# Zero fills of a decode backward kernel: waiting for the query weight instead of the output weight

## The chip, the cores and the metric

The kernel runs on one core of a Trainium2 chip. The metric is the device time of one execution in microseconds (us), as the median of several executions. Of the kernel before, three runs were known at first (765.28 to 765.92 us, median 765.66); more were taken later beside every experiment, on the same chip as that experiment. A run more than 1.5% above the fastest of the same kernel is called slow, and comparisons use the other (fast) runs alone.

## The reference, cut to what matters

The program is forward and backward of a decode step: layer norm, attention over the last 4096 positions of a 32768-long cache, multiplied by a gated feed-forward branch. It returns the output and nine gradients.

```python
k_cache, v_cache: bf16 [2, 8, 32768, 128]
W = 4096                                     # only the last W positions are attended to
k = k_cache[:, :, Sk - W:, :]; v = v_cache[:, :, Sk - W:, :]
s = attention(xn @ wq, k, v) @ wo            # xn = layernorm(x)
g = silu(square(relu(xn @ w1 + b1)) @ w2 + b2)
out = x + s * g
return out, gradients for (x, k_cache, v_cache, wq, wo, w1, b1, w2, b2)
```

What matters is the size of the outputs. The gradients of both caches are 134 MB each, and seven eighths of each is exact zero, because only the last 4096 of 32768 positions were used. The kernel therefore has to write some 235 MB of zeros, beside about 46 MB of other outputs and 46 MB of inputs.

## The kernel before

The zeros come from one zeroed tile `zt` in on-chip memory. There are 32 zero areas (2 gradients, 2 batch entries, 8 heads), each of 28672 x 128 bf16, 7.34 MB. GpSimd issues 31 of them through its software DMA queue ("fills"), and SyncE issues the last one at the very end.

```python
ZR = SK - W                                   # 28672 zero rows per area
def zf(o, q, r0, nent, rows, rep=1):          # one fill: nent partitions, rows rows per packet
    ...
    sw_fill.append(nc.gpsimd.dma_start(out=v, in_=zs))

zlong = (0, 1, 3, 5, 7, 11, 12, 16, ..., 30)  # these areas go in packets of 224 rows = 57344 B
zshort = {2: (...), 4: (...), ...}            # eight areas cut by hand into smaller pieces
...
for qi in range(ZQ - 1):
    r = 0
    whole = (P, ZR // P, 1) if qi in zlong else (P, ZG, ZR // (P * ZG))   # 57344 B or 28672 B
    for n, rows, rep in zshort.get(qi, (whole,)):
        r = zf(*zparts[qi], r, n, rows, rep)
```

The loads are issued by SyncE, in this order, and the first fill waits for one of them:

```python
dma_load.dma_start(out=w1, ...)                        # 1.8 MB, feed-forward weights
dma_load.dma_start(out=w2, ...)                        # 1.8 MB
wo_in = dma_load.dma_start(out=wo[:], ...)             # 4.2 MB, output weight
dma_load.dma_start(out=wq[:], ...)                     # 4.2 MB, query weight
vnat = load(A_v_cache, 0, "v")                         # 4.2 MB, first V tile
# ... the fills are issued here, by GpSimd ...
for f in sw_fill:
    tc.add_manual_dep(f.ins, wo_in.ins.name, ...)      # every fill waits for wo
```

The compute chain is: layer norm, feed-forward branch, transposes of `wo`, queries (the first use of `wq`), then four rounds. A round uses a V tile and a K tile of 4.2 MB each; their gradients overwrite them in place and are stored by ScalarE's DMA queue, and only after that store has landed can the next V or K tile be loaded into the same memory. So loads, stores and compute of the rounds form one long chain. The first K load waits for compute to have read `w1` and `w2`, whose memory it takes. The end:

```python
dma_store.dma_start(out=out_5..., in_=wo[:])           # gradient of wo
...
nc.sync.dma_start(out=out_8..., in_=dw2_st)
...
last = nc.sync.dma_start(out=out_6..., in_=dw1_st)     # last result of compute, 1.8 MB
with tc.issue_after(last.ins):
    fin = nc.sync.dma_start(out=v, in_=zs)             # the 32nd zero area, 7.34 MB
tc.add_manual_dep(fin.ins, sw_fill[-2].ins.name, ...)  # and it waits for the last fill but one
```

Of the kernel before, what the change touches and what calls it, by code (L numbers as in the profile page):

```python
# [16 lines left out]
def kernel(  # L17
# [34 lines left out]
    DK = D // P  # L52
    NJ = N // P
# [14 lines left out]
    dma_load = nc.sync  # L68
# [104 lines left out]
    wq = wts.tile([P, DK, N], BF16, name="wq")  # L173
    wo = wts.tile([P, NJ, D], BF16, name="wo")
# [33 lines left out]
    def load(src, r, tag):  # L208
        nat = kvp.tile([P, NCB * DH], BF16, tag=tag)
        dma_load.dma_start(out=nat[:], in_=kv_of(src, r))  # L210
        return nat[:].rearrange("p (c d) -> p c d", d=DH)

    with tc.tile_pool(name="pw", bufs=1) as pw:
# [7 lines left out]
        dma_store.dma_start(out=b2_bf[:], in_=B_b2.rearrange("(p k) -> p k", k=DK))  # L221
        dma_load.dma_start(out=w1, in_=B_w1.rearrange("(p k) f -> p k f", k=DK))
        dma_load.dma_start(out=w2, in_=B_w2.rearrange("(p j) d -> p j d", j=FK))
        wo_in = dma_load.dma_start(out=wo[:], in_=A_wo.rearrange("(p j) m -> p j m", j=NJ))
        dma_load.dma_start(out=wq[:], in_=A_wq.rearrange("(p k) n -> p k n", k=DK))
        vnat = load(A_v_cache, 0, "v")
        for qi in range(ZQ - 1):
            r = 0
# [2 lines left out]
                r = zf(*zparts[qi], r, n, rows, rep)  # L231
            assert r == ZR
        for f in sw_fill:
            tc.add_manual_dep(f.ins, wo_in.ins.name,
                              mybir.DependencyInfo(mybir.DependencyClass.Sync, mybir.DependencyReason.DATA))

        tp = ps_m.tile([P, DK, B], BF16, tag="m")
# [66 lines left out]
        for j0 in range(0, NJ, JG):  # L304
            woT = pw.tile([P, JG, DK, P], BF16, tag="woT", bufs=2)
            for half in range(2):
                tp = ps_t.tile([P, 8, P], BF16, tag="pt")
                for jj in range(8):
                    j, dk = divmod(half * 8 + jj, DK)
# [31 lines left out]
        for g0 in range(0, len(jobs), 8):  # L341
# [4 lines left out]
            j = 0  # L346
            while j < len(grp):
                dst, idx, off = grp[j][1], grp[j][2], grp[j][3]
                n = 1
# [83 lines left out]
    for r in range(NR):  # L433
# [122 lines left out]
        for hk in range(h0, h0 + NP) if b == B - 1 else ():  # L556
            xps = ps_m.tile([P, DK, B], F32, tag="m")
            for half in range(2):
                wqT = wsl.tile([P, 2, DK, P], BF16, tag="wqT")
                tp = ps_t.tile([P, 8, P], BF16, tag="pt")  # L560
                for jj in range(8):
                    i, k = divmod(half * 8 + jj, DK)
# [51 lines left out]
    for k in range(DK):  # L614
        for n0 in range(0, F, 512):
            n = min(512, F - n0)
# [58 lines left out]
```

## Time and profile before

| | before |
|---|---|
| median of the first three runs | 765.66 us |
| span of the profiled run | 764.6 us |
| bytes moved, mean rate | 326.73 MB, 427 GB/s |
| first fill issued | 23.1 us |
| last result of compute handed to the DMA | 696.9 us |
| last fill issued (by SyncE) | 724.2 us |

The first lines are from the page: the span, the busy times, the shares of the span in 40 equal slices (a digit is tenths; the GB/s row is the rate of each slice), the totals, and the DMA queues (packets, MB, share of the 16 engines).

```profile
span 764.6 us, 9391 instructions
...
PE 388.6 (51%) x4109; PEld 234.4 (31%) x4118; DVE 275.8 (36%) x483; ACT 214.9 (28%) x313; POOL 34.7 (5%) x67
...
DMA  9999999999999999999999999999999999999998
GB/s 378 434 410 428 447 420 425 442 438 414 437 423 435 429 435 431 426 433 425 430 430 445 430 422 438 422 436 424 440 442 430 430 425 432 432 427 428 442 409 367
DMA packets 12217, 326.73 MB, mean 427 GB/s; under 512 B 2898, under 2 KB 2906, under 8 KB 2934
...
q0 software_dynamic: 7744, 227.55, 70.3%
q1 hardware_dynamic: 2696, 56.63, 20.8%
q10 hardware_dynamic: 1736, 41.95, 13.9%
```

The DMA row has no hole, and from the 2nd to the 38th of the 40 slices the rate stays between 410 and 447 GB/s. q0 is the fills, q1 what SyncE issues (loads, some stores, the last fill), q10 what ScalarE issues (stores). No compute engine is near its limit. The view of stretches says the same of the end; its columns are the stretch, its length, busy time (and instructions) of PE, PE's weight loads, VectorE, ScalarE and GpSimd, then the granted clock, the DMA share and GB/s (a transfer counts where it starts, so a share can pass 1):

```profile
700.00:745.00 45.00, 0.00 (x0) 0.00 (x0) 0.00 (x0) 0.00 (x0) 0.00 (x0) 0.50 1.02 427
745.00:760.00 15.00, 0.00 (x0) 0.00 (x0) 0.00 (x0) 0.00 (x0) 0.00 (x0) 0.50 1.01 433
```

For the last 60 us no compute engine does anything, and the pipe (here: the 16 DMA engines taken together) is full almost to the end. So compute ends long before the kernel does.

The wait that the change moves is in the view of waits of GpSimd (who waited for whom: us in total, times, longest):

```profile
POOL out_dram L101 <- DMA out_dram<-zt: 507.8, 39, 27.3
...
POOL out_dram L101 <- DMA wo<-in_A_wo_dram: 21.4, 1, 21.4
```

The first line is the normal course of the fills: each new one waits for room behind an earlier one. The second is the wait for `wo` at the start. In the timeline (start us, us, engine, line, operation) the first eight fills follow at once, and the end is in SyncE's queue:

```profile
23.08 4.83 POOL L101 DMA_DIRECT2D out_dram<-zt  x8 [21.43 <-DMA wo<-in_A_wo_dram]
...
696.91 0.33 SPq L639 DMA_DIRECT2D out_dram<-dw  x1
724.24 0.39 SPq L644 DMA_DIRECT2D out_dram<-zt  x1
```

The DMA view gives KB of one transfer and the median us from issue to landing:

```profile
out_dram<-nat ACTq DMA_DIRECT2D x8, 4096.0 KB, 40.5
...
nat<-in_A_v_cache_dram SPq DMA_DIRECT2D x4, 4096.0 KB, 31.8
nat<-in_A_k_cache_dram SPq DMA_DIRECT2D x4, 4096.0 KB, 26.6
...
wq<-in_A_wq_dram SPq DMA_DIRECT2D x1, 4096.0 KB, 41.2
```

The query weight was issued at 2.2 us (timeline) and landed 41.2 us later, at about 43.4 us, because from 27.5 us on it shared the engines with fills.

### The profile page before, as it was taken

What the parts mean: (1) busy time and instruction counts of PE and PEld (TensorE: products, weight loads), DVE (VectorE), ACT (ScalarE), POOL (GpSimd) and SP (SyncE); (2) the same over time, 40 slices, a digit from 0 to 9 for tenths busy, and PEclk for the clock granted to TensorE, in tenths of its full rate; (3) what the DMA queues carried; (4) which work ended last, traced back from release to release, by engine and by line L of the source; (5) the groups of instructions that cost most, each with busy time, mean ns of one, the idle gap of its engine ahead of it and who ended that gap; (6) DMA issues with size and microseconds to landing.
All of it is one profiled execution on the core that took longest, in us unless ns stands there. A gap on an engine that the chain in (4) does not pass through costs nothing.

```text
span 764.6 us, 9391 instructions
## 1 busy us (share of the span) xinstructions
PE 388.6 (51%) x4109; PEld 234.4 (31%) x4118; DVE 275.8 (36%) x483; ACT 214.9 (28%) x313; POOL 34.7 (5%) x67
## 2 busy tenths in 40 slices
PE   0566774477007747830784770038459467594000
PEld 0543553333005534410463320026344333321000
DVE  3234342485003446430554650014344245663000
ACT  0044521455001246530224550002422254153000
POOL 0200100010000000000000000000000000000000
PEclk9986997778556867665596775559859666555555
DMA  9999999999999999999999999999999999999998
GB/s 378 434 410 428 447 420 425 442 438 414 437 423 435 429 435 431 426 433 425 430 430 445 430 422 438 422 436 424 440 442 430 430 425 432 432 427 428 442 409 367
DMA packets 12217, 326.73 MB, mean 427 GB/s; under 512 B 2898, under 2 KB 2906, under 8 KB 2934
## 3 DMA queue, kind: packets, MB, share of 16 engines
q0 software_dynamic: 7744, 227.55, 70.3%
q1 hardware_dynamic: 2696, 56.63, 20.8%
q10 hardware_dynamic: 1736, 41.95, 13.9%
q8 instruction: 32, 0.52, 0.3%
q14 instruction: 9, 0.07, 0.0%
HBM read 45.62 MB, written 280.50 MB: 427 GB/s over the span
## 4 chain that ended last, share of the span: by engine, by line
DMA 32%; PE 31%; DVE 13%; ACT 9%; issue 6%; ACTq 0%; SPq 0%; DVEq 0%
DMA out_dram<-nat 14%; DMA nat<-in_A_v_cache_dram 8%; DMA nat<-in_A_k_cache_dram 7%; PE tp L387 6%; PE ov L421 5%; ACT tring L150 3%; DMA b_bf<-in_B_b_dram 2%; ACT p_bf L455 2%; ACT nat L150 2%; DVE tring L152 2%; PE s_ps L394 2%; DVE nat L152 2%; DVE ds_bf L468 2%; PE wps L588 2%; PE dops L314 2%
## 5 line engine op out<-in xcount | busy, mean ns | idle before, releaser
L387 PE MATMUL tp<-pperm,nat 128*128 128x128 bf16 x1024 | 91.9, 243 | 144.7 <-DMA nat<-in_A_v_cache_dram 126.5
L152 DVE COPY tring<-tp 128x1024 bf16<-128x1024 bf16 (+1 forms) x98 | 65.9, 689 | 179.1 <-PE tp L387 169.4
L387 PEld LDWEIGHTS <-nat 128*128 128x128 bf16 x1024 | 68.5, 109 | 165.1 <-DMA nat<-in_A_v_cache_dram 128.4
L150 ACT CAST nat<-ov 128x512 bf16<-128x512 f32 x160 | 87.7, 589 | 68.8 <-PE ov L421 48.1
L150 ACT COPY tring<-tp 128x1024 bf16<-128x1024 bf16 (+1 forms) x34 | 34.4, 1011 | 228.5 <-PE tp L387 155.1
L152 DVE CAST nat<-ov 128x512 bf16<-128x512 f32 x96 | 65.6, 690 | 59.7 <-PE ov L421 57.1
L101 POOL DMA_DIRECT2D out_dram<-zt x58 | 33.1, 576 | 529.3 <-DMA out_dram<-zt 507.8
L421 PE MATMUL ov<-bd,ds_bf 128*128 128x512 bf16 x124 | 49.4, 472 | 6.6 <-DVE nat L152 3.9
L421 PE MATMUL ov<-bd,p_bf 128*128 128x512 bf16 x123 | 47.3, 451 | 5.5 <-DVE nat L152 1.4
L410 PE MATMUL ps<-t,nat 128*128 128x16 bf16 x1024 | 28.7, 173 | 14.3 <-DVE bd L375 7.2
L410 PEld LDWEIGHTS <-nat 128*128 128x128 bf16 x1024 | 28.7, 103 | 17.1 <-issue 11.9
L394 PEld LDWEIGHTS <-zz 128*32 128x32 bf16 x512 | 17.8, 96 | 33.4 <-issue 23.1
L152 DVE CAST wq<-wps 128x512 bf16<-128x512 f32 x16 | 11.0, 690 | 42.4 <-PE wps L581 42.3
L402 PE MATMUL tp<-ident_bf,p_bf 128*128 128x128 bf16 x64 | 7.6, 312 | 34.9 <-ACT p_bf L455 34.9
L394 PE MATMUL s_ps<-tring,zz 128*32 128x256 bf16 x256 | 19.2, 288 | 11.8 <-ACT tring L150 7.4
L394 PE MATMUL dp_ps<-tring,zz 128*32 128x256 bf16 x256 | 20.5, 326 | 7.1 <-ACT tring L150 4.2
L150 ACT CAST wq<-wps 128x512 bf16<-128x512 f32 x16 | 9.4, 586 | 51.7 <-PE wps L581 51.7
L455 ACT ACTIVATE p_bf<-e_sb,rl 32x512 bf16<-32x512 f32 x16 | 22.8, 1424 | 3.4 <-DVE rl L452 3.2
L468 DVE SCALAR_TENSOR_TENSOR ds_bf<-dp_ps,delta,p_bf 32x512 bf16<-32x512 f32 x16 | 21.7, 1355 | 0.2
L421 PEld LDWEIGHTS <-ds_bf 128*128 128x128 bf16 x128 | 13.1, 110 | 20.6 <-issue 18.3
L421 PEld LDWEIGHTS <-p_bf 128*128 128x128 bf16 x128 | 12.9, 110 | 19.6 <-issue 16.7
L564 PE MATMUL tp<-ident_bf,wq 128*128 128x128 bf16 x128 | 16.8, 248 | 2.3 <-issue 2.3
(195 smaller groups left out, 435.5 us busy)
## 6 DMA issues: line engine op xcount, KB each, us to landing
out_dram<-zt POOLq DMA_DIRECT2D x23, 7168.0 KB, 100.0
out_dram<-nat ACTq DMA_DIRECT2D x8, 4096.0 KB, 40.5
out_dram<-zt POOLq DMA_DIRECT2D x7, 3584.0 KB, 71.3
nat<-in_A_v_cache_dram SPq DMA_DIRECT2D x4, 4096.0 KB, 31.8
nat<-in_A_k_cache_dram SPq DMA_DIRECT2D x4, 4096.0 KB, 26.6
out_dram<-zt SPq DMA_DIRECT2D x1, 7168.0 KB, 39.5
out_dram<-zt POOLq DMA_DIRECT2D x2, 3488.0 KB, 66.9
out_dram<-zt POOLq DMA_DIRECT2D x1, 6120.0 KB, 67.6
```

Of the source, the lines that this page charges most:

```text
L101: sw_fill.append(nc.gpsimd.dma_start(out=v, in_=zs))
L150: nc.scalar.copy(out=out_ap, in_=in_ap)
L152: nc.vector.tensor_copy(out=out_ap, in_=in_ap)
L314: nc.tensor.matmul(dops[0:B, :, :], lhsT=dsT_bf[:, dk, :], rhs=woT[:, :, dk, :], start=(dk == 0), stop=(dk == DK - 1))
L387: nc.tensor.transpose(tp[:, j, :], nat[:, g * CC + half * CH + j, :], pperm[:].rearrange("p b k -> p (b k)"))
L394: nc.tensor.matmul(out_ps[pr * RB:(pr + 1) * RB, half * CH * PB:(half + 1) * CH * PB], lhsT=zbuf[:, pr, o:o + RB], rhs=tT[:, :, pr, :], st ...
L410: nc.tensor.matmul(ps[:], lhsT=nat[:, g * CC + half * CH + cc, :], rhs=cols[half][:, cc, :, g, :], start=(half == 0 and g == 0 and cc == 0 ...
L421: nc.tensor.matmul(ov[:], lhsT=src[:, cc].rearrange("r k b -> r (k b)"), rhs=bd[:, gh * 4:(gh + 1) * 4, :], start=True, stop=True)
L455: nc.scalar.activation(out=p_bf[rb, :, :, pr], in_=e_sb[rb], func=ACT.Copy, scale=rl[rb, 0:1])
L468: nc.vector.scalar_tensor_tensor(out=ds_bf[rb, :, :, pr], in0=dp_c[rb], scalar=delta[rb, 0:1], in1=p_bf[rb, :, :, pr], op0=ALU.subtract, o ...
L564: nc.tensor.transpose(tp[:, jj, :], wq[:, k, n0:n0 + DH], ident_bf[:, :])
L588: nc.tensor.matmul(wps[:], lhsT=o_rows[:, j:N:NJ], rhs=ds_rows[:, :], start=True, stop=True)
```

## The change

The intent is to let one more load have the pipe to itself before the flood of zeros starts. One wait moves; no instruction is added, removed or reordered on any engine.

```diff
-        wo_in = dma_load.dma_start(out=wo[:], in_=A_wo.rearrange("(p j) m -> p j m", j=NJ))
-        dma_load.dma_start(out=wq[:], in_=A_wq.rearrange("(p k) n -> p k n", k=DK))
+        dma_load.dma_start(out=wo[:], in_=A_wo.rearrange("(p j) m -> p j m", j=NJ))
+        wq_in = dma_load.dma_start(out=wq[:], in_=A_wq.rearrange("(p k) n -> p k n", k=DK))
         vnat = load(A_v_cache, 0, "v")
 ...
         for f in sw_fill:
-            tc.add_manual_dep(f.ins, wo_in.ins.name,
+            tc.add_manual_dep(f.ins, wq_in.ins.name,
                               mybir.DependencyInfo(mybir.DependencyClass.Sync, mybir.DependencyReason.DATA))
```

## The prediction

> **What bounds the kernel now.** The DMA engines, from the first microseconds to the last. The page shows the DMA row at 9 tenths in 39 of 40 slices, and 326.73 MB at a mean 427 GB/s: 326.73 MB / 427 GB/s = 765 us, the whole span (764.6). Compute is far from that: PE 51%, VectorE 36%, ScalarE 28%. The view of stretches shows every compute engine at zero from 700 us on, while the DMA keeps moving 400 to 443 GB/s until 750 us. The chain of waits is mixed (DMA 32%, PE 31%) and doesn't set the end: the last store (a 7168 KB zero fill issued by SyncE at 724 us) shares a full pipe. The Trainium skill, "DMA: Bandwidth & Descriptors", section "Issuing engines are not separate DMA queues", says that transfers started by any engine run on the same 16 DMA engines and interleave; the trace agrees: the total stays near 430 GB/s whichever queues are active.
>
> **What the change does.** No instruction is added, removed or reordered; one semaphore wait before the first GpSimd fill moves from the output weight to the query weight. Before, GpSimd waited 21.4 us for the output weight and issued its first fill at 23.1 us; fill data moved from about 27.5 us. From there fills shared the engines with the loads of the query weight (landed at about 43 us, 2.2 + 41.2) and the first V tile (65 to 75 us).
>
> After, loads keep the engines alone longer, at about 425 GB/s: the query weight (12.06 MB of loads in all) should land near 32 us, the first fill be issued at 32 to 34 us, fill data start at 36 to 38 us, and V land at 44 to 50 us.
>
> **What is on the critical path.** Almost nothing. The queue is not empty in the moved interval: behind the query weight stands the 4.2 MB load of V, which covers the roughly 10 us by which fills come later. 10 us at 425 instead of 431 GB/s costs about 0.1 us (estimate). By about 75 us both kernels have moved the same bytes. Compute doesn't gain: the query weight is first read at 73.8 us, V after 95 us; the first K load waits for PE until about 95 us; the output weight, first read at 37.2 us, comes no earlier. The start of the fills costs a dip (352, 327 and 364 GB/s in the three microseconds from 25 us, about 0.6 us of pipe); it should move to about 34 to 37 us, as large.
>
> **Prediction.** 765.7 us, 8 times in 10 between 764.5 and 767.0. Faster by over 2%: 1%; within 2%: 98%; slower by over 2%: 1%.
>
> **What would show it.** First fill at 32 to 34 us in the timeline; query weight landing about 10 us earlier; the dip moved; mean rate still 426 to 428 GB/s; last compute still near 697 us; GpSimd's fills ending near 746 us with the SyncE fill after them.
>
> **What would make it wrong.** Loads running dry before fills arrive (a dip of several us between 30 and 45 us) would add up to 4 us. A changed phase between fills, loads and stores could change the unequal finish of the 16 DMA engines in the last 3 us, worth perhaps 1 us either way. If the dip at the start of the fills vanished because fewer loads are queued, 0.6 us would be gained. Compute would have to slip by some 30 us to show in the end.

## The result, and the profile after

| | before | after |
|---|---|---|
| median, 6 runs each, same chip | 765.51 us | 765.40 us |
| range | 765.24 to 765.92 | 765.14 to 765.74 |
| ratio, 95% interval | | 0.9998, 0.9985 to 1.0011 |
| first fill issued | 23.1 us | 32.7 us |
| query weight landed | 43.4 us | 32.0 us |
| last result of compute handed over | 696.9 us | 693.3 us |

Here and below, a ratio is the mean time of one kernel's fast runs over the mean of the other's in the same rounds, so it is not quite the ratio of the medians.

The time is the same. The page of after, the same lines:

```profile
span 763.9 us, 9400 instructions
...
DMA  9999999999999999999999999999999999999998
GB/s 381 428 427 415 452 416 424 446 432 419 431 426 433 431 441 432 416 431 434 432 426 437 433 428 429 433 428 430 438 430 431 436 423 440 432 428 430 436 416 375
DMA packets 12217, 326.73 MB, mean 428 GB/s; under 512 B 2898, under 2 KB 2906, under 8 KB 2934
```

The view of waits of GpSimd, the two lines that answer to those of before:

```profile
POOL out_dram L101 <- DMA out_dram<-zt: 497.9, 39, 27.4
POOL out_dram L101 <- DVE h2T_bf L275: 31.0, 1, 31.0
```

GpSimd waited 31.0 instead of 21.4 us at the start and 9.9 us less later: the wait was moved from the course of the fills to their beginning. (The second line names a VectorE instruction as releaser. No fill reads `h2T_bf`; as built, the first fill waits for the load's semaphore and for the zero tile. The view infers releasers, and this is a case where it picked the wrong one. In runs e7 and e8 below, which have this same gate, it names the load of `wq`, with 31.1 and 30.8 us.)

The timeline and the DMA view of after:

```profile
32.66 4.84 POOL L101 DMA_DIRECT2D out_dram<-zt  x8 [31.00 <-DVE h2T_bf L275]
...
693.25 0.33 SPq L639 DMA_DIRECT2D out_dram<-dw  x1
724.41 0.39 SPq L644 DMA_DIRECT2D out_dram<-zt  x1
```

```profile
out_dram<-nat ACTq DMA_DIRECT2D x8, 4096.0 KB, 41.2
...
nat<-in_A_v_cache_dram SPq DMA_DIRECT2D x4, 4096.0 KB, 32.3
nat<-in_A_k_cache_dram SPq DMA_DIRECT2D x4, 4096.0 KB, 26.7
...
wq<-in_A_wq_dram SPq DMA_DIRECT2D x1, 4096.0 KB, 29.8
```

The query weight came 11.4 us earlier, the fills 9.6 us later, and the first V tile, which stands behind the query weight, 17.2 us earlier (76.5 and 59.3 us by the last completion record). The last result of compute came 3.7 us earlier, which gained nothing. The individual DMA records of the two traces (each has a queue, a size, a start and a duration) can be added up; with the bytes of each record spread evenly over its duration, they give this:

```
MB moved since the start        40 us   50 us   60 us   75 us   95 us
before, all queues              15.73   20.04   24.34   30.83   39.40
before, fills alone              3.60    6.45    8.94   14.49   23.03
after, all queues               15.77   20.09   24.41   30.90   39.47
after, fills alone               0.81    3.76    8.08   14.55   23.10

GB/s in steps of 1 us (from)      24   25   26   27   28
before                           415  352  327  364  428
                                  33   34   35   36   37   38
after                            433  396  358  332  374  425
```

At 40 us the changed kernel is 2.8 MB of fills behind and as much ahead in loads; the sum is the same at every time. At 75 us the fills are level too. From there on the two kernels are the same program with the same bytes moved, within 0.1 MB. The small dip at the start of the fills moved with them and kept its size: 0.64 us of pipe time in both, against 432.5 GB/s.

### The profile page after: what moved, and what is told of

Read it like the earlier page. It is cut to its first block, busy times and chain, and to the rows that moved or that the text cites. A ratio compares the mean times of both kernels' runs of the same rounds, so it can differ in the third digit from the quotient of the medians.

```text
span 763.9 us, 9400 instructions
## 1 busy us (share of the span) xinstructions
PE 386.4 (51%) x4118; PEld 233.1 (31%) x4118; DVE 275.6 (36%) x483; ACT 214.8 (28%) x313; POOL 34.7 (5%) x67
## 2 busy tenths in 40 slices
DMA packets 12217, 326.73 MB, mean 428 GB/s; under 512 B 2898, under 2 KB 2906, under 8 KB 2934
## 4 chain that ended last, share of the span: by engine, by line
DMA 32%; PE 31%; DVE 13%; ACT 9%; issue 6%; ACTq 0%; DVEq 0%; SPq 0%
DMA out_dram<-nat 15%; DMA nat<-in_A_k_cache_dram 11%; PE ov L421 7%; PE tp L387 5%; DMA nat<-in_A_v_cache_dram 4%; ACT p_bf L455 2%; DMA b_bf<-in_B_b_dram 2%; ACT nat L150 2%; ACT tring L150 2%; PE ps L410 2%; PE s_ps L394 2%; DVE nat L152 2%; DVE ds_bf L468 2%; DVE tring L152 2%; PE wps L588 2%
## 5 line engine op out<-in xcount | busy, mean ns | idle before, releaser
L421 PE MATMUL ov<-bd,p_bf 128*128 128x512 bf16 x128 | 49.2, 457 | 4.3 <-ACT nat L150 1.4
L394 PEld LDWEIGHTS <-zz 128*32 128x32 bf16 x512 | 17.7, 96 | 33.9 <-issue 23.8
## 6 DMA issues: line engine op xcount, KB each, us to landing
out_dram<-nat ACTq DMA_DIRECT2D x8, 4096.0 KB, 41.2
nat<-in_A_k_cache_dram SPq DMA_DIRECT2D x4, 4096.0 KB, 26.7
```

What stands on the lines that cost most here:

```text
L394: nc.tensor.matmul(out_ps[pr * RB:(pr + 1) * RB, half * CH * PB:(half + 1) * CH * PB], lhsT=zbuf[:, pr, o:o + RB], rhs=tT[:, :, pr, :], st ...
L421: nc.tensor.matmul(ov[:], lhsT=src[:, cc].rearrange("r k b -> r (k b)"), rhs=bd[:, gh * 4:(gh + 1) * 4, :], start=True, stop=True)
```

## The experiments

Twelve kernels were run, all of them variants of the changed kernel. Theory A is that of the prediction: the pipe is full from start to end, so time is bytes over rate, and the place of the gate is worth nothing as long as there are other transfers queued. Rivals: the time is set by when compute starts (B); small shifts never show because compute has slack (C); loads alone on the pipe are better than loads mixed with fills (D).

### e1: no gate at all

```diff
-        for f in sw_fill:
-            tc.add_manual_dep(f.ins, wq_in.ins.name, ...)
```

> No zero fill waits for any weight; the first one waits only for its zero tile (about 5 us). Theory A (a full pipe: time is bytes over rate, the gate's place is worth nothing as long as the pipe never runs dry): 765.4 us, within 1 us of after; first fill issued near 5 us, output weight lands 10 to 20 us later than 23 us, last compute 5 to 20 us later than in after (693 us), which slack swallows. Rival B (the gate earns its keep by getting weights in early, and compute's start sets the end): slower by the delay of the output weight, 8 to 20 us, so 773 to 785 us.

Measured: 766.21 us median; five of six runs between 766.09 and 766.29, one at 792.01. Ratio of the fast runs to before 1.0008 (0.9995 to 1.0021). The first fill was issued at 4.9 us. The DMA records have the last data of the output weight at 50.7 us, 29 us later than in after (21.9 us), more than I had expected; the first K load came 21 us later (117.0 against 96.2 us), and the last result of compute 7.5 us later (700.8 against 693.3 us). So compute was held up a good deal and the fast runs show nothing of it: rival B is out. The single slow run was a surprise, and is taken up again with e6.

### e2: gate on the last load in the queue

```diff
-            tc.add_manual_dep(f.ins, wq_in.ins.name, ...)
+            tc.add_manual_dep(f.ins, tile_in[0].ins.name, ...)   # the first V tile
```

> The fills wait for the first V tile, the last load in the queue. Theory A: nothing is queued behind V, so the pipe stands idle from V's landing (about 40 us) to the first fill data, some 4.5 to 5 us (0.5 us to issue, 4.4 us from first issue to first data as before and after show); the dip at the start of the fills (0.6 us) goes. Time 769.5 us, between 768 and 771. Rival C (the place of the gate never matters, slack swallows a few us): 765.4 within 0.7. Rival D (loads alone on the pipe are better, so a later gate is better): under 764.5.

Measured: 768.81 us (five runs, 768.73 to 769.43), ratio 1.0044 (1.0032 to 1.0056). Slower, as theory A says (0.4%, far under the 2% mark, but clear of the noise), and rivals C and D are out: a hole of 4 us early on shows in full although compute has slack of over 40 us. The hole, in the view of stretches of e2 (columns as above):

```profile
40.00:44.00 4.00, 2.73 (x22) 1.38 (x21) 0.69 (x1) 2.56 (x2) 0.98 (x2) 1.00 0.06 25
44.00:48.00 4.00, 3.26 (x19) 1.90 (x19) 1.46 (x1) 1.59 (x2) 3.84 (x7) 0.61 1.07 459
```

The excess is a little smaller than the 4.1 us expected. From the DMA records, 3.65 us of pipe time were lost around the hole, instead of the 0.64 us of after's dip; the difference, 3.0 us, stands against 3.4 us measured. The step of my estimate that was off is the start of the fills: with loads queued the first fill data came 4.4 us after the first issue (before and after alike), but on an empty pipe they came after 1.2 us (issued at 43.02, data at 44.26 us).

### e3: the same gate, but with a load behind it

The gate is on V, as in e2, and V is loaded before the query weight, which then stands in the queue behind it.

```diff
-        wq_in = dma_load.dma_start(out=wq[:], ...)
         vnat = load(A_v_cache, 0, "v")
+        wq_in = dma_load.dma_start(out=wq[:], ...)
```

> The same gate on V as e2_gate_v, but V is loaded before the query weight, so that 4.2 MB of load stand behind it. Theory A: covered again, 765.4 us within 1 us, first fill near 32.7 us, a dip like after's near 35 us. If waiting for V as such cost something (a later start of compute or another order of fills), this run would be as slow as e2_gate_v, about 769.5.

Measured: 765.67 us (765.22 to 766.14), ratio 1.0001 (0.9989 to 1.0013). First fill at 33.4 us. The 3.4 us of e2 are gone, though the fills wait for the same tile. So it's not what the fills wait for, but whether 4.2 MB of other work is queued behind it. That is why the change itself was free: its gate has V behind it.

### e4: the same hole, ten times as long

```diff
-            tc.add_manual_dep(f.ins, wq_in.ins.name, ...)
+            tc.add_manual_dep(f.ins, do_in.ins.name, ...)   # a copy of compute near 76 us
```

> The fills wait for a late copy of compute (the output gradient's transposed heads, near 77 to 80 us). Theory A: the pipe is empty from 40 us to about 82 us, 38 to 44 us of idle that nothing gives back: 803 to 810 us. Rival C: much of it is swallowed by slack (compute has some 45 us): under 790.

Measured: 803.16 us (801.48 to 804.00), ratio 1.0488 (1.0475 to 1.0502). Stretches of e4:

```profile
44.00:48.00 4.00, 3.18 (x18) 1.72 (x18) 1.28 (x1) 1.67 (x2) 0.00 (x0) 0.59 0.00 0
48.00:75.00 27.00, 16.91 (x113) 9.37 (x111) 11.05 (x11) 12.06 (x9) 0.00 (x0) 0.75 0.00 1
```

The records give 38.2 us of pipe time lost, 37.5 more than after's dip; the time rose by 803.16 - 765.40 = 37.8 us. One microsecond of empty pipe cost about one microsecond, in this hole as in the short one of e2. Both lie before 80 us.

### e5: fewer bytes

One 7.34 MB area isn't filled, so its output is wrong.

```diff
         for qi in range(ZQ - 1):
+            if qi == 12:
+                continue
```

> One of the zero fills of 7.34 MB is left out (the result is wrong on purpose there, if the buffer isn't zero by luck). Theory A: time falls by its bytes over the rate, 7.34 MB / 432 GB/s = 17.0 us, to 748.4 us (747.5 to 749.5). Rival B (compute and its loads set the end): under 8 us.

Measured: 748.40 us (748.27 to 748.69), ratio 0.9777 (0.9764 to 0.9789). Against 765.65 us of before in the same rounds this is 17.25 us less, for 7.34 MB / 432 GB/s = 17.0 us. Bytes set the time.

### e6 and e7: compute starts later

The first mean is computed 11 or 31 times instead of once. Nothing else changes.

```diff
-        bsum(meanb[:], xT_f)
+        for _ in range(1 + 10):          # e7: 1 + 30
+            bsum(meanb[:], xT_f)
```

> The first mean is computed eleven times instead of once, so that all compute starts some 22 to 25 us later, with the bytes unchanged. Theory A: 765.4 us within 1.5 us, last compute near 715 to 720 us. Rival B: slower by up to 22 us.

> As e6_late10, with the mean computed 31 times: compute starts some 65 to 75 us later. Theory A: the slack of compute, about 45 us in after (693 us to the last compute; then 1.8 MB of store and 7.3 MB of fill at 432 GB/s still have to follow, 21 us; 763 - 693 - 21 = 49), is used up; 780 to 795 us, with the pipe running below 430 GB/s in the last 60 us. Rival B: 830 us. If time stays at 765, the slack was underrated.

e6 measured: four of seven runs from 765.86 to 766.49 us (ratio of these 1.0009, 0.9994 to 1.0023), and three from 786.90 to 789.81. The fast runs agree with theory A. The profile fell into a slow run, so no reading is rested on it.

e7 measured: 836.03 us (four runs, 834.75 to 837.56), ratio 1.0922. I had expected 780 to 795, and this is a miss. The pipe ran dry near the end; the page of e7:

```profile
DMA  9999999999999999999999999999999993147179
GB/s 382 439 435 409 448 416 434 433 432 425 429 435 434 431 431 427 434 437 427 440 423 437 420 431 443 428 425 436 430 442 427 437 435 139 53 203 302 51 333 396
```

In e7 the first K load was issued at 154.2 us, 58 us later than in after, but the last result of compute was handed over at 810.5 us, 117 us later (693.3 in after). The slip doubled on its way through the rounds. My estimate of the slack was not the fault: from the last result to the end e7 needed 834.3 - 810.5 = 23.8 us, so in a kernel of 764 us compute may end as late as 740 us, 47 us later than it does in after. What failed is the assumption that a late start carries through unchanged.

The DMA records show what the late loads met. All are loads of 4.2 MB, in 128 packets of 32768 B; the six are V and K of the second to fourth rounds. "Completion" is the duration of the slowest of the load's 4-byte completion records, which follow the data. The rows of fills give the share of fill time beside the load that is spent in large packets:

```
                                    V1    K1    V2    K2    V3    K3
after: data, us                   23.4  20.6  26.0  18.6  22.9  18.2
after: fills in 57344 B packets     0%    0%    0%    0%   17%    0%
after: completion, us              0.0   0.0   0.0   0.1   0.0   0.0
e7: data, us                      20.4  20.1  31.8  16.1  32.4  26.2
e7: fills in 57344 B packets       28%    0%   98%   22%  100%  100%
e7: completion, us                 0.0   0.0   2.2   4.5   2.2  12.7
```

In after, these loads run beside fills in small packets, V3 in part excepted. The list of areas with small packets is an arrangement in time: they come up just when the kernel loads. In e7 compute is late, and three of the loads fall on large packets. Theory E is that large packets make loads slow, in two ways. A load of 32768 B packets that takes turns with fill packets of 57344 B gets 32768 / (32768 + 57344) = 36% of the pipe, beside 28672 B packets 53%. And its completion records wait for fill packets: over e7 and e11 (below) their long durations cluster at 2.16, 4.27, 8.49, 10.6, 12.7 and 14.8 us, multiples of a step of 2.11 us, against 2.13 to 2.16 us for nine in ten of the 57344 B packets themselves. The Trainium skill, "DMA: Bandwidth & Descriptors", section "Queues, rings and completion order", states both halves: an engine goes round its queues and switches only at packet boundaries, and the semaphore increment is an ordered write that lands only after every earlier write from that engine, across its queues. The trace agrees with both, with the numbers above; neither kernel shows which writes a completion waited for, so the second half rests on the steps. Beside small packets nearly all completion records are short (e8 to e10), though fills are being written there too; why is not shown. Nor does the theory explain the first K load, which the table leaves out: in e7 it took 26.7 us with a completion of 14.8 us (89% of the fill time beside it in large packets), but in after 18.2 us with a completion of 0.0, although 72% was in large packets there too.

### e8 to e11: packet size alone

```diff
-    zlong = (0, 1, 3, 5, 7, 11, 12, 16, 17, 18, 19, 22, 23, 24, 25, 26, 27, 28, 29, 30)
+    zlong = ()                       # e8 (with e6's delay), e9 (with e7's delay), e10 (no delay)
+    zlong = tuple(range(ZQ))         # e11 (no delay), and zshort = {}
```

> As e6_late10 (compute some 20 us late; 3 of its 7 runs took 787 to 790 us, the others 766), but every large fill goes in packets of 28672 B instead of 57344 B for most. New theory E: an engine takes packets of its queues in turn, so a load beside 57344 B fill packets gets less of the pipe, and its completion writes wait for fill packets already started (whole multiples of 2.12 us in the trace); the kernel before keeps small packets in place just when its late loads run, and a slip of compute of 20 us moves the loads into large ones. Expected by E: all runs within 1.5 us of 766, none near 788; late loads 17 to 26 us of data and completion writes at most 5 us. Rival F (the slow mode is a state of the chip or clock, not of the packets): some runs near 788 again.

> As e7_late30 (836 us; expected 780 to 795), with the small packets of e8. Theory E: compute slips rigidly by the 58 us by which the first K load came later (154.2 against 96.2 us), so that it ends near 751 us and the kernel near 770 to 790 us. Rival G (compute stretches under late fills for other reasons): 820 us or more.

> The changed kernel with small fill packets everywhere and nothing else moved. Theory A and E: 765.4 us within 1.2 us, for the pipe stays full. If large packets were there because small ones move fewer bytes per us, slower by several us.

> The changed kernel with 57344 B packets in all fills, the eight specially cut ones included; compute is not delayed. Theory E: the six late loads take 26 to 32 us of data instead of 18 to 26, and their completion up to 15 us more, some 50 to 100 us over the three rounds; compute ends near 745 to 790 us and the kernel takes 775 to 815 us. Rival F: 765.4 us, as after.

| run | compute delayed | large fill packets | first K load issued | last result of compute | median us (range) | ratio |
|---|---|---|---|---|---|---|
| after | no | mixed | 96.2 | 693.3 | 765.40 (765.14 to 765.74) | 0.9998 |
| e7 | 31 means | mixed | 154.2 | 810.5 | 836.03 (834.75 to 837.56) | 1.0922 |
| e10 | no | none | 98.9 | 653.0 | 765.96 (765.80 to 766.45) | 1.0006 |
| e8 | 11 means | none | 117.7 | 677.8 | 767.08 (766.68 to 767.50) | 1.0018 |
| e9 | 31 means | none | 155.9 | 729.9 | 766.94 (766.64 to 767.53) | 1.0018 |
| e11 | no | all | 95.8 | 812.9 | 838.82 (826.35 to 840.28) | 1.0873 |

Theory E holds for what the packets of the fills do to the loads and to the time, and more strongly than I had put it. With small packets everywhere the 836 us of e7 become 766.9 us in e9 at the same delay. With large packets everywhere the kernel is 61 and 73 us slower in its two fast runs (826.35 and 838.57 us; the other two, 839.08 and 840.28, count as slow, and the ratio leaves them out) with no delay at all, though it moves the same MB, in fewer packets (8968 against 12217). (e11 also does away with the eight areas cut by hand; e7 and e9 differ in the packets of the whole areas alone.) The DMA view of e10, and then of e11 (KB, median us to landing; stores of the rounds, V loads, K loads):

```profile
out_dram<-nat ACTq DMA_DIRECT2D x8, 4096.0 KB, 28.7
...
nat<-in_A_v_cache_dram SPq DMA_DIRECT2D x4, 4096.0 KB, 29.3
nat<-in_A_k_cache_dram SPq DMA_DIRECT2D x4, 4096.0 KB, 25.3
```

```profile
out_dram<-nat ACTq DMA_DIRECT2D x8, 4096.0 KB, 54.4
nat<-in_A_v_cache_dram SPq DMA_DIRECT2D x4, 4096.0 KB, 40.7
nat<-in_A_k_cache_dram SPq DMA_DIRECT2D x4, 4096.0 KB, 48.3
```

Loads and stores are both slower by far in e11. The second K load, which runs beside fills alone, took 18.2 us for its data in e10 and 25.9 us in e11: 4.194 MB / 18.2 us = 230 GB/s and 162 GB/s, against 53% and 36% of 432 GB/s, which are 229 and 157. (All four K loads: 17.3 to 18.5 us in e10, 24.4 to 28.4 in e11.) Its completion then took up to 14.8 us more in e11.

My expectations were off in two places. e9 was put at 770 to 790 us, and e11 at 775 to 815. For e9 I had let the delay of 58 us start from after's compute; but small packets alone bring the end of compute from 693.3 to 653.0 us (e10), with faster stores (28.7 instead of 41.2 us) and slightly faster loads, and from there a delay of 57 us ends at 729.9 us, still before the 740 us that compute may take. For e11 I had counted the loads and not the stores.

e10 is also the cleanest test of theory A: compute ended 40 us earlier and the kernel gained nothing (ratio 1.0006, 0.9993 to 1.0018). Stretches of e10:

```profile
655.00:690.00 35.00, 0.00 (x0) 0.00 (x0) 0.00 (x0) 0.00 (x0) 0.00 (x0) 0.50 1.02 434
```

None of the five runs of e8 was slow, where three of seven were in e6. The granted clock of e6's slow runs, 0.705 to 0.710, lies within that of its fast ones, 0.705 to 0.715, so a lower clock doesn't set them apart. This fits theory E (the slow runs would be those in which the slip met large packets and grew), but five runs are few, and no fast profile of e6 was taken to set against the slow one; how the slow runs of e6 and e1 come about is thus made likely and not shown.

### e12: no gate, small packets

e1 and e10 together: both edits above.

> No wait in front of the fills, as e1_no_gate (766.2 us, with one of six runs at 792), and small fill packets as in e10. Theory A and E: 766.0 to 767.0 us, no run near 790, last compute earlier than in e1 (700.8 us). If the gate is worth something on its own, over 768 us or a slow run. Five runs can't exclude a rare slow one.

Measured: 767.31 us (five runs, 766.87 to 767.94), ratio 1.0021 (1.0008 to 1.0035), no slow run. The time is 0.3 us above the range that I gave. The first slice of the page has 360 GB/s instead of after's 381, but that is mostly the dip at the start of the fills (266 GB/s at the lowest, between 7 and 11 us), which after has at 34 to 38 us. By the DMA records e12 is behind after by 0.8 us of pipe time at 19 us, by 0.3 us at 45 us, and by 1.3 us at 600 us: most of the excess is lost slowly, over the whole run. e8 and e9, with small packets too, are also 1.2 to 1.3 us above before of the same rounds, with intervals that exclude 1. The cause of these small losses is open. Compute ended at 664.7 us and was no matter. No version beat the two kernels: the medians of all of those with a full pipe and all bytes lie between 765.4 and 767.3 us.

## Why the prediction was right

- **"What bounds the kernel now: the DMA engines, from the first microseconds to the last."** Right. e5 took bytes away and gained their time (17.25 us for 17.0), e4 put a hole in and paid for it (37.8 us for 37.5), and e10 made compute 40 us faster for nothing.
- **"The queue is not empty in the moved interval."** Right, and the decisive step. e2 and e3 have the same gate, once with nothing and once with 4.2 MB queued behind it: 768.81 and 765.67 us.
- **"By about 75 us both kernels have moved the same bytes."** Right: 30.83 and 30.90 MB, and of fills 14.49 and 14.55 MB. Later experiments show that this matters more than I knew. Since the fills are level again before the first K load, the small packets still meet the loads of the rounds. A change that shifted compute against the fills would have put that at risk.
- **Times of the events.** First fill 32.7 us (32 to 34 predicted), query weight near 32.0 us (near 32), first fill data at 37.0 us (36 to 38), dip from 34 to 38 us with the same 0.64 us (34 to 37 us, about 0.6), last compute 693.3 us (697 within some us), GpSimd's fills ending at 746.7 us (near 746). For V the predicted 44 to 50 us holds for the data (48.7 us by the records) but not for the completion, which waited until 59.3 us; nobody needed V before 95 us.
- **"10 us at 425 instead of 431 GB/s costs about 0.1 us."** Too small to be tested; the interval of the ratio is wider.
- **"Compute would have to slip by some 30 us to show in the end."** This is the weak point, though it didn't decide the case. As a figure for the end of compute it is on the safe side (47 us by e7's tail). As a figure for a delay early in the kernel it is wrong: in e7 58 us became 117, while in e9, with other packets, 57 us became 77 and stayed hidden.

## What to carry to other kernels

When the DMA engines are full from start to end, ask of every wait only one thing: is something else queued while it lasts? Here moving a wait was free if so, and cost about the empty time if not (3.4 us for 3.0, 37.8 us for 37.5), although compute had slack. And the size of the packets of a background transfer isn't neutral even when the rate is: in e10 and e11 it changed the share, and the completion delay, of the loads that the compute chain waits for, so a kernel can be tuned to an alignment in time that a later change breaks without touching it.

## What the Trainium skill lacked or had wrong

- "DMA: Bandwidth & Descriptors", section "Queues, rings and completion order", says that engines take turns by packet, but not what this does to shares: a load of 32768 B packets got 230 GB/s beside 28672 B fill packets and 162 GB/s beside 57344 B ones, at the same total of about 432.
- The same section states that the completion write lands after all earlier writes of the engine. It gives no size of the delay: here up to 14.8 us after the data, in steps of 2.11 us beside 57344 B packets, and mostly under 0.1 us beside small ones (the longest were 6.7 us for a load in e9 and 13.0 us for a store in e12).
- "DMA: Bandwidth & Descriptors", section "Where 436 GB/s comes from", says that for transfers between HBM and SBUF the HBM side (about 358 GB/s) binds. That sentence leaves out a condition that stands beside the page's table of measured loads: with the other core of the pair idle, one core reached 425 GB/s. In this kernel, on one core, the limit doesn't bind either: 427 to 428 GB/s over the whole kernel and 431 to 434 in many slices, with 280 of 327 MB being writes.
- The same page, section "Latency and other measured facts", gives about 1 us to the first byte of a GpSimd-issued transfer. On an empty pipe the trace has 1.24 us from first issue to first data (e2), but 4.4 us with loads queued in the engines (before and after; e1, without a gate, too).
- No page has the dip at the start of GpSimd's fills while loads are in flight: down to 327 GB/s for some 3 us, 0.64 us of pipe time in both kernels. Its cause stays open.
